# One matmul of 512 columns where the hi and the lo half of a weight matrix took two of 256

## The chip, the cores and the metric

The kernel runs on one core of a Trainium2 chip. The metric is the device time of one execution in microseconds (us). TensorE is called PE in the profile, VectorE DVE, ScalarE ACT, GpSimd POOL, and SyncE SP.

## What is computed

Three layers follow one another on 8 x 3072 tokens of 256 features. The third is the one that the change touches.

```python
X = np.fft.rfft(x, axis=1); y = np.fft.irfft(X * F, n=S, axis=1)     # 1: filter along the tokens
e = argmax(x @ w_gate); out[i] = gate * (relu(x[i] @ w1[e]) @ w2[e]) # 2: 8 experts, capacity 768
h = x @ w_in                                                         # 3: 256 -> 2048
g = np.maximum(h, 0.0) + np.log1p(np.exp(-np.abs(h)))                #    softplus
return g @ w_out                                                     #    2048 -> 256
```

## The kernel before

Only tokens that get one of the 6144 places of layer 2 need layers 2 and 3 in full. They are worked through in 16 **units** of 384 tokens (8 experts, two halves each); `units[v]` is unit v. Matrix products of layers 2 and 3 are done three times, in a 4-byte matmul format called fp32r: every operand is split into a part hi and a rest lo, and hi x hi, hi x lo and lo x hi are summed in PSUM.

For each unit the third layer runs over KI = 16 **chunks** of 128 hidden features. `wi(i)` makes the pre-activation `pi` of chunk i (six matmuls of 384 columns). ACT takes Abs, Exp and Ln of it, DVE adds `max(h, 0)` (`g`), ACT rounds to `gh`, and POOL subtracts to get `gl`. `wo(i)`, four steps later, multiplies with the chunk's 256 columns of `w_out`: for each of the three groups of 128 tokens (t = 0, 1, 2) it runs gh x woh, gh x wol and gl x woh, nine matmuls of 256 columns. They sum into `po` over all 16 chunks. `po` lies in two PSUM banks (pool `pso`): tokens t = 0 and 1 in the two halves of the first, t = 2 in the second. After chunk 15 `take` copies the three sums to SBUF tiles `ot` on DVE, and `store` scatters them to the output from POOL's queue. The next unit's `wo(0)` writes the same two banks, so its first matmul waits for `take`.

The program is one list of steps. Unit v's chunk i has step 16 v + i, and events of one step are put out in the order W2, WI, SP, WO, SUM, W1, TAKE. Between `wo(15)` of a unit (step 16 v + 19) and `wo(0)` of the next (step 16 v + 20) PE therefore runs one `w1` block (`pw`), one `w2` block (`py`) and one `wi` block (`pi`), each of six matmuls of 384 columns; these `w1` and `w2` blocks belong to the second layer of later units. DVE gets `hl`, the rest that belongs to that `w1` block, ahead of `take`. From unit 13 on no `w1` or `w2` is left, and only `wi` lies between.

`P.pv` is another PSUM pool, of one bank. It is scratch space of the conversion of `w_in` and `w_out` (`split_res`) and idle after that.

Of the kernel before, what the change touches and what calls it, by code (L numbers as in the profile page):

```python
# [7 lines left out]
F32 = mybir.dt.float32  # L8
F32R = mybir.dt.float32r
# [3 lines left out]
ALU = mybir.AluOpType  # L13
# [4 lines left out]
NB, S, D, E = 8, 3072, 256, 8  # L18
# [183 lines left out]
def body(tc, cap, x, ff, fx, wg, w1, w2, win, wout, m1, m2, m3, m4, small, out):  # L202
    nc = tc.nc
# [5 lines left out]
    KI = DFF // 128  # L209
# [10 lines left out]
    pso = ctx.enter_context(tc.tile_pool(name="pso", bufs=2, space=PSUM))  # L220
# [18 lines left out]
    ts = const.tile([128, nblk], F32, name="ts")  # L239
# [352 lines left out]
    def left_pools(st, tag):  # L592
        pool = lambda n, b: st.enter_context(tc.tile_pool(name=tag + n, bufs=b, reuse_waits="tile"))
        P.g = pool("g", 4)
        P.sp = pool("sp", 3)
        P.o = pool("o", 7)
        wp = pool("wo", 1)
        P.woh = wp.tile([128, KI, D], F32R, name="woh")
        P.wol = wp.tile([128, KI, D], F32R, name="wol")

    def load_res(q, which):
        t = P.wl.tile([128, 512], mybir.dt.int64 if f64 else F32, name="wst", tag="wst", bufs=3)
# [3 lines left out]
    def split_res(q, which, space):  # L606

        t = P.res.pop((q, which))  # L610

        def parts():
            if which == 0:
                return (w[q].rearrange("p b k f -> p (b k f)") for w in (P.wih, P.wil))
            return (w[:, 2 * q:2 * q + 2].rearrange("p b c -> p (b c)") for w in (P.woh, P.wol))

        if f64:
            two = t.bitcast(U32).rearrange("p (f two) -> p f two", two=2)
            lw, hw = two[:, :, 0], two[:, :, 1]
            if space is None:  # L620
                v = P.wl.tile([128, 512], U32, name="wv", tag="wv", bufs=1)
            else:
                pool, tag = space()
                v = pool.tile([128, 512], U32, name="pv", tag=tag)
            f = P.wl.tile([128, 512], F32, name="wf", tag="wf")
            nc.vector.tensor_scalar(v, hw, 0xFFFFF, 0x100000, op0=ALU.bitwise_and, op1=ALU.bitwise_or)
            nc.vector.scalar_tensor_tensor(out=f, in0=lw, scalar=2.0 ** -32, in1=v, op0=ALU.mult, op1=ALU.add)
            nc.vector.tensor_scalar(v, hw, 0x7FF00000, None, op0=ALU.bitwise_and)
            yield 0
            nc.scalar.activation(out=v, in_=v, func=ACTF.Relu, scale=8.0, bias=ebias)  # L630
            yield 1
            nc.vector.scalar_tensor_tensor(out=v, in0=hw, scalar=0x80000000, in1=v,
                                           op0=ALU.bitwise_and, op1=ALU.bitwise_or)
            nc.vector.scalar_tensor_tensor(out=f, in0=f, scalar=2.0 ** -20, in1=v.bitcast(F32),
                                           op0=ALU.mult, op1=ALU.mult)
            yield 2
        else:
            f = t
            yield 0
            yield 1  # L640
            yield 2
        hi, lo = parts()
        nc.scalar.copy(hi, f)
        yield 3
        nc.gpsimd.tensor_tensor(out=lo, in0=f, in1=hi.bitcast(F32), op=ALU.subtract)
# [17 lines left out]
    class Unit:  # L663
# [148 lines left out]
            self.sp_h(i)  # L812
            self.sp_l(i)

        def wo(self, i):
            if i == 0:
                po = [pso.tile([128, 2, D], F32, name="po", tag="o") for _ in range(2)]
                self.po = [po[0][:, 0], po[0][:, 1], po[1][:, 0]]
            gh, gl = self.g.pop(i)
            for t in range(3):  # L820
                ts = slice(t * 128, t * 128 + 128)
                for n, (a, b) in enumerate(((gh, P.woh), (gh, P.wol), (gl, P.woh))):
                    nc.tensor.matmul(self.po[t], lhsT=a[:, ts], rhs=b[:, i], skip_group_check=True,  # L823
                                     start=(i == 0 and n == 0 and t != 1), stop=(i == KI - 1 and n == 2))

        def take(self):
            self.ot = []
            for t in range(3):
                ot = P.o.tile([128, D], F32, name="ot", tag="ot")
                nc.vector.tensor_copy(ot, self.po[t])  # L830
                self.ot.append(ot)

        def store(self, group, tiles=range(3)):
# [9 lines left out]
    class Rest:  # L843


        def sums(self, k, c):
            if not k and not c:
                self.s = P.o.tile([128, 2, D], F32, name="cs", tag="cs", bufs=1)
            cs = slice(32 * c, 32 * c + 32)
            src = (P.woh, P.wol)[k].bitcast(F32)[:, :, cs].rearrange("p k c -> p c k")  # L850
            nc.vector.tensor_reduce(out=self.s[:, k, cs], in_=src, axis=AXL.X, op=ALU.add)

        def zero(self):
# [21 lines left out]
    with tc.manual_schedule():  # L875
# [17 lines left out]
        units = [Unit(e, h) for h in range(nunit) for e in range(E)]  # L893
# [46 lines left out]
        for g in range(8):  # L940
            for h in range(2):
                n = "x1", g, h
                add(n, "PE", 896, lambda g=g, h=h: cv.x1(0, g, h), after=["m1", "warm", ("x", 0, g)],
                    take=["a", "e1"] if g + h == 0 else ["a"], give=[("xt", ("x", 0, g))],
# [4 lines left out]
        for k in range(12):  # L949
            n = "tr1", k  # L950
# [3 lines left out]
        for b in range(1, STATIC):  # L954
            for g in range(8):
                for i in range(2):
                    n = "xo", b, g, i
                    add(n, "PE", 856, lambda b=b, g=g, i=i: cv.x1_out(b, g, i), after=["m1", ("x", b, g)],
                        take=["a"] if i else ["a", "s1"], give=[("xt", ("x", b, g))], behind=[("xo", b, g, 0)] if i else [])
# [10 lines left out]
        for b in range(STATIC):  # L970
            for k in range(12):
                s2, tf, zs, s3, se = (("s2", b, k // 2), *((x, b, k) for x in ("tf", "zs", "s3", "se")))
                prev = lambda x, n=12, k=k: [(x, b, k - 1)] if k else [(x, b - 1, n - 1)] if b else []
                if k % 2 == 0:
# [7 lines left out]
                    take=["o"] if k else ["o", f"e{b % 2}"], give=[("z", tf)], behind=prev("s3"))  # L982
# [3 lines left out]
            for h in range(2):  # L986
                n = "gs", b, h
                add(n, "PE", 1000, lambda b=b, h=h: cv.gsum(b, h), after=es + ["const"], take=["o"], give=[e0])
                add(("gx", b, h), ("DVE", "ACT")[h], 520, lambda b=b, h=h: cv.gsum_x(b, h), after=[n],
                    take=["gx"] if h == 0 else [], give=[("o", n)], behind=[("gx", b, 0)] if h else [])  # L990
            for t in range(2):
                n = "gt", b, t
# [3 lines left out]
                    take=["gsb"] if t == 0 else [], give=[("a", n)], behind=[("gg", b, 0)] if t else [])  # L996
# [34 lines left out]
            for m in range(16):  # L1031
# [7 lines left out]
                    take=["o"] if m % 2 else ["o", "yt"], give=[("j", tr)], behind=prev("s4"))  # L1039
# [43 lines left out]
        def left_room():  # L1083
            stl.close()
            left_pools(stm, "M")
# [9 lines left out]
        W2, WI, SP, WO, SUM, W1, TAKE, TR, AHEAD = range(9)  # L1095
# [21 lines left out]
        for v in range(HEAD):  # L1117
            u = units[v]
# [4 lines left out]
            for k in range(2):  # L1123
                n = "pt", v, k
# [5 lines left out]
            for j in range(8):  # L1130
                if v > 1 and 16 * (v - 2) + 2 * j - 3 >= STEPS:
                    continue
                n = "w1", v, j
                add(n, "PE", 1044, lambda u=u, j=j: u.w1_p(j), after=[("xl", v, 0), ("xl", v, 1), ("wl", v, j // 2)],
                    take=["a"], give=[("x", ("xh", v, 0)), ("w1h", ("wh", v, j // 2))],
# [3 lines left out]
                if v < 2 or 16 * (v - 2) + 2 * j < STEPS:  # L1139
# [3 lines left out]
                        take=["yy", "yy"] if j == 0 else [],  # L1143
                        give=[("h", ("hh", v, j)), ("w2h", ("wh", v, 4 + j // 2))], tail=2000)
            for d in range(2 if ("w2", v, 7) in plan.node else 0):
                add(("yh", v, d), "ACT", 490, lambda u=u, d=d: u.y_h(d), after=[("w2", v, 7), "low"],
                    take=["Y"] if d == 0 else [], behind=[("yh", v, 0)] if d else [])
# [7 lines left out]
        for n, (q, which) in enumerate(res):  # L1155
            kind = (n >= TURN[0]) + (n >= TURN[1])
            tag = "yov"[kind]
# [11 lines left out]
        def prior(*n):  # L1169
            return [n] if n in plan.node else []  # L1170

        for v, u in enumerate(units):
            for i in range(KI):
                t = 16 * v + i
                wi, ab, su, gh, gl, wo = ((x, v, i) for x in ("wi", "ab", "su", "gh", "gl", "wo"))
                if t < STEPS:
                    add(wi, "PE", 1044, lambda u=u, i=i: u.wi(i), after=[("yl", v, 0), ("yl", v, 1), ("c", i // 2, 4), "left"],
                        take=["a"], give=[("Y", ("yh", v, 0))], behind=prior("wi", *((v, i - 1) if i else (v - 1, KI - 1))))
# [5 lines left out]
                if t + 4 < STEPS:  # L1184
                    add(wo, "PE", 1075, lambda u=u, i=i: u.wo(i), after=[gl, ("c", KI // 2 + i // 2, 4)],
                        take=["o"] * 2 * (i == 0), give=[("gg", gh)],
# [21 lines left out]
        def ev(t, order, fn, *args):  # L1208
            if t < STEPS:
                return  # L1210
            at.setdefault(t, []).append((order, len(at.get(t, ())), fn, args))
# [19 lines left out]
        for v, u in enumerate(units):  # L1231
            b = 16 * (v - 2)
            if v >= HEAD:
                ev(b - 16, AHEAD, load_x, u)
                for k in range(2):
                    ev(b - 7 + 2 * k, TR, u.tr_x, k)
            for j in range(8 if v > 1 else 0):
                ev(b + 2 * j - 3, W1, u.w1, j)
                ev(b + 2 * j, W2, u.w2, j)
            for i in range(KI):  # L1240
                t = 16 * v + i
                ev(t, WI, u.wi, i)
                ev(t + 2, SP - 0.5, u.sp_split, i)
                ev(t, SP, u.sp_act, i)
                ev(t, SUM, u.sp_sum, i)
                ev(t + 4, WO, u.wo, i)
            ev(16 * v + 19, TAKE, u.take)
            for t in range(3):
                ev(max(16 * v + 21, 46 + 3 * v) + t * (v < len(units) - 1), AHEAD, u.store, "out", [t])
            ev(16 * v + 13, AHEAD, nc.gpsimd.drain)  # L1250
# [15 lines left out]
    with tc.If(fv > 0):  # L1266
# [53 lines left out]
        with ExitStack() as st:  # L1320
            wi_pools(st, "G")
            right_pools(st, "G")
            low_pool(st, "G")
            left_pools(st, "G")
            for k in range(2):
                for q in range(KI // 2):
                    load_res(q, k)
                    for _ in split_res(q, k, None):
                        pass
            with tc.For_i(0, E, 1) as e:  # L1330
                with tc.For_i(0, nunit, 1) as h:
                    u = Unit(e, h)
# [77 lines left out]
```

## Time and profile before

| | |
|---|---|
| time, median of 3 runs | 1044.64 us (1044.56 to 1045.86) |
| profiled execution | 1043.66 us, of which its span is 1041.9 us |
| PE busy | 1023.2 us, 98% of the span, 7112 matmuls |
| ACT, POOL, DVE busy | 777.7, 597.1, 468.1 us |
| granted PE clock, mean | 0.999 of full speed |
| `po` matmuls (L823) | 3 x 768 of 256 columns |
| `ot` copies (L830) | 48, 17.2 us in all |

The chain that ended last goes through PE for 90% of the span. Matmuls overlap in the pipeline, so the duration of one (282 ns for 256 columns) says little; what one costs a busy PE is read from the distance between starts.

### The profile page before, as it was taken

The numbers are of one execution on the slowest core, as the hardware profiler recorded it, in microseconds if no ns is written. First come the engines' busy times: TensorE is split into PE (matmuls) and PEld (weight loads), VectorE is DVE, ScalarE is ACT, GpSimd is POOL, SyncE is SP. The second block draws the span as 40 slices with busy tenths as digits, with TensorE's granted clock in tenths as the row PEclk, the third lists the DMA queues.
The fourth block names the chain that finished last, engine by engine and source line by source line (L and its number), as shares of the span: only waits on it lengthen the run. The fifth ranks groups of instructions, "written<-read, shape, count | busy, mean of one in ns | idle before, by whom it ended". The sixth has DMA issues, their size and how long they took to land.

```text
span 1041.9 us, 19044 instructions
## 1 busy us (share of the span) xinstructions
PE 1023.2 (98%) x7112; PEld 951.2 (91%) x7112; DVE 468.1 (45%) x895; ACT 777.7 (75%) x1612; POOL 597.1 (57%) x560
## 2 busy tenths in 40 slices
PE   9999999999999999999999999999999999999997
PEld 7655676699999999999999999999999999999996
DVE  3855899888856332323233333232333333322222
ACT  4465568778877787878787878787878787877885
POOL 0502544688754658665656565656565656554554
PEclk9999999999999999999999999999999999999999
DMA  9967727654211662333323333321121212100000
GB/s 291 297 214 235 246 87 249 220 178 137 71 47 41 203 258 83 135 107 112 122 92 122 111 102 112 122 92 61 51 63 51 64 51 66 46 11 6 17 16 19
DMA packets 72823, 120.04 MB, mean 115 GB/s; under 512 B 6928, under 2 KB 46736, under 8 KB 72720
## 3 DMA queue, kind: packets, MB, share of 16 engines
q1 hardware_dynamic: 65424, 96.69, 28.9%
q0 software_dynamic: 4608, 12.59, 3.5%
q10 hardware_dynamic: 2688, 9.44, 2.7%
q8 instruction: 58, 0.95, 0.4%
q14 instruction: 45, 0.37, 0.1%
HBM read 71.51 MB, written 47.19 MB: 114 GB/s over the span
## 4 chain that ended last, share of the span: by engine, by line
PE 90%; POOL 2%; DMA 2%; issue 2%; DVE 2%; ACT 1%; POOLq 0%; ACTq 0%; DVEq 0%; SPq 0%
PE pi L791 24%; PE po L823 24%; PE pw L737 13%; PE py L766 12%; PE p L437 3%; PE p L385 2%; PE p L332 2%; PE p L398 2%; PE p L309 1%; PE p L357 1%; POOL gl L808 1%; DMA xt<-in_x_dram 1%; PE pt L714 1%; PE p L536 1%; DMA fi<-in_fx_dram 1%
## 5 line engine op out<-in xcount | busy, mean ns | idle before, releaser
L657 DVE SCALAR_TENSOR_TENSOR g<-pi,ln 128x384 f32<-128x384 f32 x256 | 142.4, 557 | 488.5 <-ACT ln L652 447.2
L808 POOL TENSOR_TENSOR gl<-g,gh 128x384 fp32r<-128x384 f32 x256 | 259.9, 1018 | 114.8 <-ACT gh L803 109.0
L823 PE MATMUL po<-woh,gh 128*128 128x256 f32 x768 | 216.5, 282 | 1.9 <-DVE ot L830 1.9
L823 PE MATMUL po<-woh,gl 128*128 128x256 f32 x768 | 216.3, 282 | 1.0 <-POOL gl L808 1.0
L823 PE MATMUL po<-wol,gh 128*128 128x256 f32 x768 | 216.0, 281 | 0.0
L649 ACT ACTIVATE ab<-pi 128x384 f32<-128x384 f32 x256 | 124.7, 487 | 119.8 <-PE pi L791 113.2
L791 PE MATMUL pi<-yh,wih 128*128 128x384 f32 x512 | 172.7, 337 | 1.0 <-DVE g L657 1.0
L791 PE MATMUL pi<-yh,wil 128*128 128x384 f32 x512 | 173.2, 338 | 0.0
L791 PE MATMUL pi<-yl,wih 128*128 128x384 f32 x512 | 173.0, 338 | 0.0
L823 PEld LDWEIGHTS po<-woh,gh 128*128 128x128 f32 x768 | 144.0, 188 | 4.3 <-ACT ab L649 2.5
L823 PEld LDWEIGHTS po<-woh,gl 128*128 128x128 f32 x768 | 144.8, 189 | 1.2 <-POOL gl L808 1.2
L823 PEld LDWEIGHTS po<-wol,gh 128*128 128x128 f32 x768 | 145.1, 189 | 0.0
L652 ACT ACTIVATE ln<-ab 128x384 f32<-128x384 f32 (+1 forms) x257 | 134.9, 525 | 8.1
L650 ACT ACTIVATE ab<-ab 128x384 f32<-128x384 f32 (+1 forms) x257 | 134.8, 525 | 8.1
L689 POOL TENSOR_TENSOR w1l<-ws,w1h 128x512 fp32r<-128x512 f32 x64 | 82.9, 1296 | 98.0 <-ACT w1h L684 68.6
L803 ACT CAST gh<-g 128x384 fp32r<-128x384 f32 x256 | 130.0, 508 | 0.7 <-DVE g L657 0.5
L689 POOL TENSOR_TENSOR w2l<-ws,w2h 128x512 fp32r<-128x512 f32 x64 | 82.9, 1296 | 74.9 <-ACT w2h L684 73.6
L791 PEld LDWEIGHTS pi<-yh,wih 128*128 128x128 f32 x512 | 96.2, 188 | 1.3 <-DVE g L657 1.3
L791 PEld LDWEIGHTS pi<-yh,wil 128*128 128x128 f32 x512 | 96.3, 188 | 0.0
L791 PEld LDWEIGHTS pi<-yl,wih 128*128 128x128 f32 x512 | 96.2, 188 | 0.0
L377 POOL TENSOR_TENSOR z<-z,t 128x512 f32<-128x512 f32 x36 | 45.8, 1273 | 75.8 <-DVE t L372 59.9
L766 PE MATMUL py<-hh,w2h 128*128 128x384 f32 x256 | 88.5, 346 | 0.0
(140 smaller groups left out, 1894.8 us busy)
## 6 DMA issues: line engine op xcount, KB each, us to landing
ws<-in_w_dram SPq DMA_DIRECT2D x128, 256.0 KB, 2.9
out_dram<-cs SPq DMA_DIRECT2D x48, 512.0 KB, 4.1
xt<-in_x_dram SPq DMA_DIRECT2D x24, 384.0 KB, 7.1
mid<-s ACTq DMA_DIRECT2D x16, 384.0 KB, 4.3
rowsd<-yt SPq DMA_DIRECT2D x16, 384.0 KB, 3.9
it<-mid SPq DMA_DIRECT2D x24, 256.0 KB, 4.4
wst<-in_win_dram SPq DMA_DIRECT2D x8, 512.0 KB, 6.0
wst<-in_wout_dram SPq DMA_DIRECT2D x8, 512.0 KB, 3.5
```

Of the source, the lines that this page charges most:

```text
L377: nc.gpsimd.tensor_tensor(out=z, in0=z, in1=t2, op=ALU.add)
L649: nc.scalar.activation(out=ab[:, :n], in_=h, func=ACTF.Abs)
L650: nc.scalar.activation(out=ab[:, :n], in_=ab[:, :n], func=ACTF.Exp, scale=-1.0)
L652: nc.scalar.activation(out=ln[:, :n], in_=ab[:, :n], func=ACTF.Ln, bias=1.0)
L657: nc.vector.scalar_tensor_tensor(out=g[:, :n], in0=h, scalar=0.0, in1=ln[:, :n], op0=ALU.max, op1=ALU.add)
L689: nc.gpsimd.tensor_tensor(out=lo, in0=self.ws.pop(i), in1=hi.bitcast(F32), op=ALU.subtract)
L737: nc.tensor.matmul(ps, lhsT=a[:, k, fs], rhs=b[:, k], start=(n == 0), stop=(n == 5))
L766: nc.tensor.matmul(self.py[d], lhsT=a[:, j % 2, ds], rhs=b, start=(j == 0 and n == 0), stop=(j == 7 and n == 2))
L791: nc.tensor.matmul(pi, lhsT=a[i // 2][:, i % 2, k], rhs=b[:, k], start=(n == 0), stop=(n == 5))
L803: nc.scalar.copy(gh, self.g[i])
L808: nc.gpsimd.tensor_tensor(out=gl, in0=g, in1=gh.bitcast(F32), op=ALU.subtract)
L823: nc.tensor.matmul(self.po[t], lhsT=a[:, ts], rhs=b[:, i], skip_group_check=True, start=(i == 0 and n == 0 and t != 1), stop=(i == KI - 1 ...
```

## The change

`woh` and `wol` become one tile `wo`, in which each chunk's 256 columns of hi are followed by its 256 columns of lo. From unit 1 on, `wo(i)` multiplies gh with both in one matmul of 512 columns and then gl with the hi half: six matmuls for nine, over as many columns. Each token group has a PSUM bank to itself, the third from `P.pv`, and its sum stands there in two halves. `take` copies the first half of a bank to `ot` and adds the second to it, on DVE; in the last unit ACT does the copy. Unit 0 keeps the nine matmuls and the plain copies.

```diff
-        P.woh = wp.tile([128, KI, D], F32R, name="woh")
-        P.wol = wp.tile([128, KI, D], F32R, name="wol")
+        P.wo = wp.tile([128, KI, 2, D], F32R, name="wo")
...
-        def wo(self, i):
-            if i == 0:
+        def wo(self, i, wide=False):
+            if i == 0 and wide:
+                po = [pso.tile([128, 2, D], F32, name="po", tag="o") for _ in range(2)]
+                self.po = po + [P.pv.tile([128, 2, D], F32, name="pq", tag="v")]
+            elif i == 0:
...
+                if wide:
+                    nc.tensor.matmul(self.po[t].rearrange("p k c -> p (k c)"), lhsT=gh[:, ts], skip_group_check=True,
+                                     rhs=P.wo[:, i].rearrange("p k c -> p (k c)"), start=(i == 0), stop=(i == KI - 1))
+                    nc.tensor.matmul(self.po[t][:, 0], lhsT=gl[:, ts], rhs=P.wo[:, i, 0], skip_group_check=True,
+                                     start=False, stop=(i == KI - 1))
+                    continue
...
-        def take(self):
+        def take(self, wide=False):
...
+                if wide:
+                    (nc.scalar.copy if self is units[-1] else nc.vector.tensor_copy)(ot, self.po[t][:, 0])
+                    nc.vector.tensor_tensor(out=ot, in0=ot, in1=self.po[t][:, 1], op=ALU.add)
+                else:
+                    nc.vector.tensor_copy(ot, self.po[t])
...
-                ev(t + 4, WO, u.wo, i)
-            ev(16 * v + 19, TAKE, u.take)
+                ev(t + 4, WO, u.wo, i, v > 0)
+            ev(16 * v + 19, TAKE, u.take, v > 0)
```

The order of all other work is the same on every engine. On PE, at the start of a unit (here unit 2; `pi` is the `wi` block ahead of it, `po` are the products with w_out), the rows before are these, with what each matmul waits for:

```order
L791 MATMUL pi<-yh,wil_1315 128x384
L823 MATMUL po<-woh,gh 128x256 [waits DVE_49,Activation_49]
L823 MATMUL po<-wol,gh 128x256
L823 MATMUL po<-woh,gl 128x256 [waits Pool_49]
L823 MATMUL po<-woh,gh 128x256
L823 MATMUL po<-wol,gh 128x256
L823 MATMUL po<-woh,gl 128x256
L823 MATMUL po<-woh,gh 128x256 [waits DVE_49]
L823 MATMUL po<-wol,gh 128x256
L823 MATMUL po<-woh,gl 128x256
```

The same place of the changed kernel (`pq` is the sum in the third bank):

```order
L792 MATMUL pi<-yh,wil_1315 128x384
L827 MATMUL po<-wo,gh 128x512 [waits DVE_49,PE_49,Activation_49]
L829 MATMUL po<-wo,gl 128x256 [waits Pool_49]
L827 MATMUL po<-wo,gh 128x512 [waits DVE_49,PE_49]
L829 MATMUL po<-wo,gl 128x256
L827 MATMUL pq<-wo,gh 128x512 [waits DVE_49,PE_49]
L829 MATMUL pq<-wo,gl 128x256
```

Two waits for DVE have become three, one for each token group. On DVE, `take` of a unit stands behind the `hl` of the `w1` block. Before:

```order
L749 SCALAR_TENSOR_TENSOR hl<-pw,hh 128x384 [waits Activation_49]
L830 COPY ot<-po 128x256 [waits PE_49]
L830 COPY ot<-po 128x256 [waits DMASW2_49]
L830 COPY ot<-po 128x256 [waits DMASW3_49,PE_49]
L657 SCALAR_TENSOR_TENSOR g<-pi,ln 128x384 [waits Activation_49,Pool_49] x2
```

And in the changed kernel:

```order
L750 SCALAR_TENSOR_TENSOR hl<-pw,hh 128x384 [waits Activation_49]
L841 COPY ot<-po 128x256 [waits PE_49]
L842 TENSOR_TENSOR ot<-ot,po 128x256 [waits DVE_49]
L841 COPY ot<-po 128x256 [waits DMASW2_49,PE_49]
L842 TENSOR_TENSOR ot<-ot,po 128x256 [waits DVE_49]
L841 COPY ot<-pq 128x256 [waits DMASW3_49,PE_49]
L842 TENSOR_TENSOR ot<-ot,pq 128x256 [waits DVE_49]
L658 SCALAR_TENSOR_TENSOR g<-pi,ln 128x384 [waits Activation_49,Pool_49] x2
```

Three instructions have become six at the same place, and each sum waits for the copy ahead of it on DVE itself.

## Rows read from the trace of the kernel before

**Rows 1.** The page's chain that ended last: shares of the span, by engine, by line

```profile
PE 90%; POOL 2%; DMA 2%; issue 2%; DVE 2%; ACT 1%; POOLq 0%; ACTq 0%; DVEq 0%; SPq 0%
PE pi L791 24%; PE po L823 24%; PE pw L737 13%; PE py L766 12%; PE p L437 3%; PE p L385 2%; PE p L332 2%; PE p L398 2%; PE p L309 1%; PE p L357 1%; POOL gl L808 1%; DMA xt<-in_x_dram 1%; PE pt L714 1%; PE p L536 1%; DMA fi<-in_fx_dram 1%
```

**Rows 2.** Stretches: busy us of PE, PEld, DVE, ACT, POOL; clock, DMA

```profile
500.00:600.00 100.00, 100.00 (x668) 99.59 (x667) 31.53 (x60) 78.28 (x165) 62.43 (x59) 1.00 0.33 113
975.00:1000.00 25.00, 25.00 (x178) 25.00 (x177) 6.63 (x12) 22.78 (x48) 13.59 (x15) 1.00 0.03 11
```

**Rows 3.** PE's waits: for whom, us in total, times, longest

```profile
PE po L823 <- DVE ot L830: 1.9, 2, 1.0
```

**Rows 4.** Timeline of PE, first matmul of each block: start, duration

```profile
602.12 0.34 PE L791 MATMUL pi<-yh,wih 128*128 128x384 f32 x1
...
603.16 0.28 PE L823 MATMUL po<-woh,gh 128*128 128x256 f32 x1
...
604.23 0.34 PE L791 MATMUL pi<-yh,wih 128*128 128x384 f32 x1
...
605.30 0.28 PE L823 MATMUL po<-woh,gh 128*128 128x256 f32 x1
...
606.36 0.34 PE L737 MATMUL pw<-xh,w1h 128*128 128x384 f32 x1
...
607.43 0.34 PE L766 MATMUL py<-hh,w2h 128*128 128x384 f32 x1
...
608.47 0.33 PE L791 MATMUL pi<-yh,wih 128*128 128x384 f32 x1
```

**Rows 5.** Timeline of DVE at the end of unit 6

```profile
614.97 1.08 DVE L830 COPY ot<-po 128x256 f32<-128x256 f32 x3
617.77 0.56 DVE L657 SCALAR_TENSOR_TENSOR g<-pi,ln 128x384 f32<-128x384 f32 x1 [1.72 <-ACT ln L652]
```

**Rows 6.** Timeline of PE at the same place

```profile
615.68 0.34 PE L791 MATMUL pi<-yh,wil 128*128 128x384 f32 x1
615.86 0.36 PE L823 MATMUL po<-woh,gh 128*128 128x256 f32 x1
616.06 0.28 PE L823 MATMUL po<-wol,gh 128*128 128x256 f32 x1
...
617.00 0.34 PE L791 MATMUL pi<-yh,wih 128*128 128x384 f32 x1
```

**Rows 7.** Timelines of DVE and PE at the end of unit 13

```profile
968.92 1.08 DVE L830 COPY ot<-po 128x256 f32<-128x256 f32 x3
...
969.81 0.36 PE L823 MATMUL po<-woh,gh 128*128 128x256 f32 x1 [0.97 <-DVE ot L830]
970.00 0.28 PE L823 MATMUL po<-wol,gh 128*128 128x256 f32 x1
...
970.95 0.34 PE L791 MATMUL pi<-yh,wih 128*128 128x384 f32 x1
...
972.00 0.28 PE L823 MATMUL po<-woh,gh 128*128 128x256 f32 x1
```

**Rows 8.** Single lines (duration min/median/max), and DVE's timeline in layer 2's gate

```profile
L830 DVE COPY ot<-po x48: 411/414/424, 302.4 to 1034.6; 128x256 f32<-128x256 f32 x48
155.43 0.41 DVE L497 TENSOR_TENSOR rk<-rk,pb 96x256 f32<-96x256 f32 x1
155.87 0.42 DVE L500 TENSOR_TENSOR v<-rk,oh 96x256 f32<-96x256 f32 x1
156.32 0.59 DVE L503 TENSOR_REDUCE ixf<-v 96x32 f32<-96x256 f32 x1
```

**Rows 9.** Timelines of DVE and POOL at the program's end

```profile
1033.88 1.09 DVE L830 COPY ot<-po 128x256 f32<-128x256 f32 x3 [2.75 <-PE po L823]
...
1034.59 1.00 POOL L835 DMA_INDIRECT out_dram<-ot,si  x1 [1.65 <-DVE ot L830]
...
1037.18 0.98 POOL L835 DMA_INDIRECT out_dram<-ot,si  x1 [0.30 <-issue]
```

More of the change, by code (lines that the diff above doesn't have):

```diff
@@ L614, in parts @@
                 return (w[q].rearrange("p b k f -> p (b k f)") for w in (P.wih, P.wil))
-            return (w[:, 2 * q:2 * q + 2].rearrange("p b c -> p (b c)") for w in (P.woh, P.wol))
+            return (P.wo[:, 2 * q:2 * q + 2, k] for k in range(2))
         if f64:
@@ L642, in split_res @@
         hi, lo = parts()
+        if which:
+            f = f.rearrange("p (b c) -> p b c", b=2)
         nc.scalar.copy(hi, f)
@@ L821, in wo @@
                 ts = slice(t * 128, t * 128 + 128)
-                for n, (a, b) in enumerate(((gh, P.woh), (gh, P.wol), (gl, P.woh))):
-                    nc.tensor.matmul(self.po[t], lhsT=a[:, ts], rhs=b[:, i], skip_group_check=True,
+                if wide:
[4 more added lines that the diff above has]
+                    continue
+                for n, (a, k) in enumerate(((gh, 0), (gh, 1), (gl, 0))):
+                    nc.tensor.matmul(self.po[t], lhsT=a[:, ts], rhs=P.wo[:, i, k], skip_group_check=True,
                                      start=(i == 0 and n == 0 and t != 1), stop=(i == KI - 1 and n == 2))
-        def take(self):
+        def take(self, wide=False):
             self.ot = []
@@ L829, in take @@
                 ot = P.o.tile([128, D], F32, name="ot", tag="ot")
-                nc.vector.tensor_copy(ot, self.po[t])
+                if wide:
[3 more added lines that the diff above has]
+                    nc.vector.tensor_copy(ot, self.po[t])
                 self.ot.append(ot)
@@ L849, in sums @@
             cs = slice(32 * c, 32 * c + 32)
-            src = (P.woh, P.wol)[k].bitcast(F32)[:, :, cs].rearrange("p k c -> p c k")
+            src = P.wo.bitcast(F32)[:, :, k, cs].rearrange("p k c -> p c k")
             nc.vector.tensor_reduce(out=self.s[:, k, cs], in_=src, axis=AXL.X, op=ALU.add)
```

## The prediction

> **What bounds the kernel now.** I read the chain that ended last first: it runs through PE for 90% of the span, and the products with w_out (L823) and with w_in (L791) hold 24% each [rows 1]. The stretches say the same of the part that the change touches: from 500 to 600 us PE is busy without a gap while ACT, the next engine, has 78 of 100 us, and late in the program, where only `wi` and `wo` are left, ACT has 22.8 of 25 [rows 2]. PE hardly waits, in all 1.9 us for `take`, in two places [rows 3]. So what the change saves on PE is saved in full, and every new wait of PE is paid in full. The reader should look for two things: the distance between matmul starts, and what PE meets at the start of a unit.
>
> **What PE pays for a chunk.** Nine matmuls of 256 columns lie between 603.16 and 604.23, the next nine between 605.30 and 606.36 [rows 4]: 1.065 us, or 118 ns each, where 256 columns at 2.4 GHz (the level that the granted clock of 1.00 in these stretches stands for) are 107 ns [rows 2]. A block of six matmuls of 384 columns takes 1.04 us when it follows another such block (602.12 to 603.16, 607.43 to 608.47), 173 ns each, where the columns alone are 160; it takes 1.07 us when it follows `wo` (604.23 to 605.30, 606.36 to 607.43) [rows 4].
>
> **Merged matmuls.** The columns stay: 3 x (512 + 256) are 9 x 256. What can go is the part of a matmul that doesn't come from columns, and the trace has no fp32r matmul of 512. The nearest rows give two ways to it: the 13 ns by which 384 columns exceed their streaming time, added to 213 ns, make 226; the line through 256 (118) and 384 (173.5) goes on to 229. I take 229, since that line rests on both widths. A chunk is then 3 x (229 + 118) = 1041 ns instead of 1065, 24 ns less. Of the 240 wide chunks (units 1 to 15), 14 stand at a boundary, which I cost as a whole below; 226 x 24 ns = 5.4 us. The bounds: a 512 as long as the two 256 that it replaces (236 ns) saves nothing; one at its bare streaming time (213 ns) saves 3 x 23 x 226 = 15.6 us.
>
> The Trainium skill's page "TensorE: Matmul & The Clock Gate", section "Back-to-back issue gap", puts a warm matmul at N/2.4 + 2.5 ns. By it a pair of 256 (2 x 109.2) against one 512 (215.8) is worth 2.6 ns, 1.8 us in all, so that hardly anything could be had by merging; the rows above differ from it, with 118 ns for 256 columns and 173 for 384.
>
> **The block behind it.** Each chunk is followed by one block of 384 columns, and that block is the slow one, 1.07 against 1.04 us [rows 4]. It is slow whether it is `wi` or `w1`, so it is not its operands but the nine short matmuls ahead of it. One place shows that this can go away: behind the chunk ahead of which PE had stood still for 0.97 us, the block takes 1.05 (970.95 to 972.00) [rows 7]. This looks like a supply of matmuls and weight loads that nine short matmuls run down and a pause, or longer matmuls, fill again. Six matmuls in a wide chunk's 1.04 us are as many as a 384 block has, so I expect most of it back: 240 x 30 ns = 7.2 us if all, 240 x 20 = 4.8 if as much as behind the pause. I take 6.0; the bounds are 0 and 7.2.
>
> **The boundary.** Here the change costs. Call T the start of `take` on DVE. Before, three copies run with starts 0.333 us apart (1.08 less one copy's 0.414, halved) [rows 5, 8]. The first matmul of the next unit waits for the two copies of the first bank, so until T + 0.333 + 0.414 = T + 0.75. It is recorded at T + 0.89 (615.86 against 614.97), but the one behind it follows after 0.20 us instead of 0.12, so it streams from about T + 0.97 [rows 5, 6]: 0.22 us pass between a copy's end and a streaming matmul. PE would have got there at T + 0.89 by itself (615.68 plus 0.18) [rows 6]. So this place has no slack today: the release comes 0.08 us late, and the chunk takes 1.14 us (615.86 to 617.00) [rows 6]. The 12 boundaries behind units 1 to 12 lie alike, T from 356.03 to 924.21, since `take` stands behind the `hl` of the `w1` block that PE itself does just ahead. Behind units 13 and 14 no such block is left, PE is there earlier and waits for the whole of it, but the first matmul again comes at T + 0.89 (969.81 against 968.92) [rows 7].
>
> After, each token group needs a copy and an add that waits for it. The gate has the same thing on 256 columns: an add with one operand in PSUM (`rk`, 0.42 us), and behind it an instruction that needs its result, which starts 0.44 to 0.45 us after it [rows 8]. So the add starts at T + 0.45 and ends 0.42 later, and the next, independent copy starts 0.335 after the add. The three adds end at T + 0.87, T + 1.65 and T + 2.44; the matmuls of the three groups may stream from T + 1.09, T + 1.87 and T + 2.66. PE needs only 0.347 us for a group (229 + 118 ns), so it waits again for the second and for the third, and ends the chunk at T + 2.66 + 0.35 = T + 3.01. Before it ended it at T + 0.89 + 1.14 = T + 2.03. That is 0.98 us for each of 14 boundaries, **13.7 us**. Nothing hides it: PE runs in order, and the `wi` behind it has to stand in the queue. Bounds: 0.85 us (a dependent start 0.03 and a release 0.02 quicker, three times or so), 11.9 us in all; 1.1 us, 15.4 us in all, if the added waits in PE's queue cost 0.05 each.
>
> DVE itself has room. Behind units 1 to 12 the next `g` starts at T + 2.80 (617.77) and waits for ACT [rows 5]; DVE is free by T + 2.4. Behind 13 and 14 `g` will be up to 0.7 us late, but what needs it is a `wo` four steps on. Unit 1's first chunk follows unit 0's plain copies and gains no wait.
>
> **The end.** The last unit's three scatters stand 1.3 us apart on POOL (1034.59 to 1037.18) and start with the first `ot` [rows 9]. Its sum has two steps now, ACT's copy and DVE's add, some 0.45 us more. But today the first copy waits for both token groups of its bank (1033.88); with a bank of its own, group 0 is released some 4 matmuls of 118 ns earlier, 0.47 us. I cost it at nothing, within 0.3 us.
>
> **The sum.** 13.7 - 5.4 - 6.0 = +2.3 us. On the profiled execution (1043.66 us, 1.0 below the median of the runs) that is 1045.9 us, on the median 1044.64 it is **1046.9 us**. This stands on the edge of what a measurement of this kernel can tell from no change, about 0.2% or 2.1 us.
>
> **Rivals.**
> *The merged matmul runs near its streaming time: faster.* If the excess over the columns is a price of the 256 and 384 widths that 512 hardly has, say 216 ns, a pair saves 20 ns: 3 x 20 x 226 = 13.6 us, and the sum is 13.7 - 13.6 - 6.0 = -5.9, 1038.7 us. It decides from 225 ns on: there 3 x 11.4 x 226 makes 7.7 us, which with the 6.0 equals the boundary. Against it speaks that the excess grows from 11 to 13 ns with the width [rows 4]. The 215.8 ns of the Trainium skill's page named above, for 512 columns, would be this case, if that figure held here while its 109.2 for 256 does not.
> *The slow block stays: clearly slower.* If it is the matmul of 256 columns just ahead, and not their number, that slows the next block, three of six remain and nothing comes back: 13.7 - 5.4 = +8.3, 1052.9 us. For it speaks that after the pause the `wo` matmuls themselves still ran at 118 to 120 ns (970.95 less 970.00, eight matmuls) [rows 7], so a full supply did not quicken them.
> *No change to be told.* With the whole 7.2 us back and 512 columns at 226 ns (33 ns a chunk, 7.5 us) the sum is 13.7 - 7.5 - 7.2 = -1.0, 1043.6 us. Nothing in the trace parts this from my own forecast; it is its lower edge.
>
> **How the numbers follow.** The forecast, all terms near their values (1043.0 to 1050.0), gets 0.56: 0.33 of it within 0.2%, 0.23 above. The slow block staying gets 0.22, all slower. The quick 512 gets 0.22, all faster. So faster 0.22, same 0.33, slower 0.45. The range takes in most of both rivals: 1040.0 to 1053.5 us leaves out the quick 512 below 218 ns, and a boundary at its upper bound together with a block that stays slow.
>
> **What the profile will show.** Right: the first three wide matmuls of a unit (L827) wait for DVE at three places, with 0.4 to 0.5 us ahead of the second and third, some 0.9 to 1.0 us a unit, and 13 us or so in PE's waits where 1.9 stood; starts of 512 columns 226 to 230 ns apart from the next matmul's; blocks of 384 behind `wo` at 1.04 us. Wrong, towards faster: 512 columns under 225 ns, or adds that start without waiting the copy out, so that the second and third group find their banks free. Wrong, towards slower: blocks behind `wo` still at 1.07, or one wait for the last add ahead of all three groups, which would hold PE until T + 2.66 with its whole 1.04 us still to do, 23 us in place of 13.7.

## The result and the profile after

The changed kernel takes **1053.51 us** (median of 6 runs, 1053.04 to 1056.9) where the kernel before takes 1044.6 (6 runs, 1043.31 to 1045.88): the ratio is 1.009, with a 95% interval of 1.0074 to 1.0105. It is slower by 8.9 us. The forecast was 1046.9, and the range ended at 1053.5. The profiled execution took 1053.66 us, its span is 1051.8 us and its mean granted clock 0.997.

The page of the changed kernel: PE's row, and the chain that ended last by engine and by line, to be held against [rows 1].

```profile
PE 1026.6 (98%) x6392; PEld 912.0 (87%) x6392; DVE 485.9 (46%) x937; ACT 780.2 (74%) x1615; POOL 596.9 (57%) x560
...
PE 90%; DVE 4%; issue 2%; ACT 1%; POOL 1%; POOLq 0%; ACTq 0%; DVEq 0%
PE pi L792 24%; PE pw L738 13%; PE py L767 11%; PE po L827 9%; PE pq L827 6%; PE po L829 5%; PE p L437 3%; PE p L385 3%; PE pq L829 3%; PE p L332 3%; PE p L357 2%; PE p L398 2%; DVE ot L841 2%; PE po L833 2%; PE p L309 1%
```

There are 720 matmuls fewer (6392 for 7112), and PE is busy for longer. DVE's share of the chain has doubled, and `ot` is now a line of it. The same stretch as in [rows 2]: busy us of PE, PEld, DVE, ACT, POOL, the granted clock and the DMA engines' share.

```profile
500.00:600.00 100.00, 99.18 (x566) 93.14 (x565) 33.05 (x64) 76.42 (x160) 63.22 (x59) 1.00 0.32 109
```

PE, which had no gap there, has one now. PE's waits name it: for whom, us in total, times, longest.

```profile
PE pq L827 <- DVE ot L842: 2.9, 14, 0.2
PE po L827 <- DVE ot L842: 2.8, 14, 0.2
PE po L827 <- ACT ab L651: 2.3, 2, 1.1
```

Where 1.9 us stood [rows 3], these are 8.0. The third row names ACT, but its two waits, behind units 13 and 14, end at T + 1.01 (T is the start of `take` on DVE, as in the prediction), where PE's first matmul starts at every boundary, 0.15 us after the first add has ended: they are waits for `ot` too. The 8.0 us are still less than what the boundaries cost, as the timelines of one of them tell. First DVE at the end of a unit, then PE (start, duration, engine, line, operation, idle time ahead of it).

```profile
619.44 0.41 DVE L841 COPY ot<-po 128x256 f32<-128x256 f32 x1
619.88 0.42 DVE L842 TENSOR_TENSOR ot<-ot,po 128x256 f32<-128x256 f32 x1
620.22 0.42 DVE L841 COPY ot<-po 128x256 f32<-128x256 f32 x1
620.67 0.42 DVE L842 TENSOR_TENSOR ot<-ot,po 128x256 f32<-128x256 f32 x1
621.01 0.42 DVE L841 COPY ot<-pq 128x256 f32<-128x256 f32 x1
621.46 0.42 DVE L842 TENSOR_TENSOR ot<-ot,pq 128x256 f32<-128x256 f32 x1
```

```profile
620.14 0.34 PE L792 MATMUL pi<-yh,wil 128*128 128x384 f32 x1
620.45 0.47 PE L827 MATMUL po<-wo,gh 128*128 128x512 f32 x1
620.75 0.28 PE L829 MATMUL po<-wo,gl 128*128 128x256 f32 x1
621.24 0.47 PE L827 MATMUL po<-wo,gh 128*128 128x512 f32 x1 [0.20 <-DVE ot L842]
621.55 0.28 PE L829 MATMUL po<-wo,gl 128*128 128x256 f32 x1
622.03 0.47 PE L827 MATMUL pq<-wo,gh 128*128 128x512 f32 x1 [0.21 <-DVE ot L842]
622.34 0.28 PE L829 MATMUL pq<-wo,gl 128*128 128x256 f32 x1
622.45 0.34 PE L792 MATMUL pi<-yh,wih 128*128 128x384 f32 x1
```

T is 619.44. The adds start at T + 0.44, 1.23 and 2.02, the last ends at T + 2.44, and the chunk ends at T + 3.01 (622.45), as it does at all 14 boundaries, within 0.01. Two matmuls of 512 columns with one of 256 between stand 0.79 us apart here, and 0.34 in an ordinary chunk (below): 0.45 us are lost ahead of the second group and as much ahead of the third. The view of waits shows only 0.20 of it, since a waiting matmul is also recorded as longer (0.47 us for 0.40) and the one before it is recorded with 0.28 us where the next can start 0.11 behind it. Distances between starts show the whole.

An ordinary chunk of the changed kernel (PE):

```profile
627.71 0.39 PE L827 MATMUL po<-wo,gh 128*128 128x512 f32 x1
627.93 0.28 PE L829 MATMUL po<-wo,gl 128*128 128x256 f32 x1
628.05 0.40 PE L827 MATMUL po<-wo,gh 128*128 128x512 f32 x1
628.28 0.28 PE L829 MATMUL po<-wo,gl 128*128 128x256 f32 x1
628.40 0.40 PE L827 MATMUL pq<-wo,gh 128*128 128x512 f32 x1
628.64 0.29 PE L829 MATMUL pq<-wo,gl 128*128 128x256 f32 x1
628.76 0.34 PE L792 MATMUL pi<-yh,wih 128*128 128x384 f32 x1
...
629.80 0.39 PE L827 MATMUL po<-wo,gh 128*128 128x512 f32 x1
```

The chunk takes 1.05 us and the block behind it 1.04, against 1.065 and 1.07 in [rows 4]. The block has come down as forecast; the chunk hardly has. In the trace's records, which are finer than the view's 10 ns, the medians over some 230 chunks are these (start to next start, ns):

| kernel | matmuls of a chunk, in order | chunk | block behind |
|---|---|---|---|
| before | 115 122 117, 118 117 118, 119 121 117 | 1063 | 1070 |
| after | 229 113, 233 117, 241 125 | 1058 | 1043 |

In units 3 to 11 one chunk is longer than that: the last one, ahead of the boundary. Here are PE and POOL there, at the end of unit 6.

```profile
616.04 0.40 PE L827 MATMUL po<-wo,gh 128*128 128x512 f32 x1
616.28 0.37 PE L829 MATMUL po<-wo,gl 128*128 128x256 f32 x1
616.49 0.40 PE L827 MATMUL po<-wo,gh 128*128 128x512 f32 x1
...
617.18 0.34 PE L738 MATMUL pw<-xh,w1h 128*128 128x384 f32 x1
```

```profile
610.06 1.29 POOL L690 TENSOR_TENSOR w1l<-ws,w1h 128x512 fp32r<-128x512 f32 x1 [2.29 <-ACT w1h L685]
...
615.19 2.00 POOL L809 TENSOR_TENSOR gl<-g,gh 128x384 fp32r<-128x384 f32 x2
```

The same place before, POOL and then PE:

```profile
605.55 1.30 POOL L689 TENSOR_TENSOR w1l<-ws,w1h 128x512 fp32r<-128x512 f32 x1 [2.29 <-ACT w1h L684]
...
610.68 2.00 POOL L808 TENSOR_TENSOR gl<-g,gh 128x384 fp32r<-128x384 f32 x2
```

```profile
611.64 0.28 PE L823 MATMUL po<-woh,gh 128*128 128x256 f32 x1
```

POOL does `w1l`, three gathers of `xd` and then two `gl`, the first of which is ready after about half of its row, at 616.2. From `w1l` to `gl` this takes 5.13 us (610.06 to 615.19), and before it took as much (605.55 to 610.68). But PE comes to this chunk 5.98 us after `w1l`'s start (616.04), where it came 6.09 us after it before (605.55 to 611.64): it has run three quicker chunks and blocks in between. The `gl` that was just in time is now late. The second matmul needs it: it is recorded at 0.37 us instead of 0.28, and the next stands 0.21 us behind it, not 0.12. The chunk takes 1.14 us (616.04 to 617.18), and 1.14 to 1.16 in each of the nine units. In units 1, 12, 13 and 14 the last chunk takes the ordinary 1.06. In unit 2 it waits over a microsecond for `gl` in both kernels, 2.34 us before and 2.43 after.

### The profile page after: what moved, and what is told of

It reads as the page before. It is cut to its first block, busy times and chain, and to the rows that moved or that the text cites. A ratio compares the mean times of both kernels' runs of the same rounds, so it can differ in the third digit from the quotient of the medians.

```text
span 1051.8 us, 17698 instructions
## 1 busy us (share of the span) xinstructions
PE 1026.6 (98%) x6392; PEld 912.0 (87%) x6392; DVE 485.9 (46%) x937; ACT 780.2 (74%) x1615; POOL 596.9 (57%) x560
## 4 chain that ended last, share of the span: by engine, by line
PE 90%; DVE 4%; issue 2%; ACT 1%; POOL 1%; POOLq 0%; ACTq 0%; DVEq 0%
PE pi L792 24%; PE pw L738 13%; PE py L767 11%; PE po L827 9%; PE pq L827 6%; PE po L829 5%; PE p L437 3%; PE p L385 3%; PE pq L829 3%; PE p L332 3%; PE p L357 2%; PE p L398 2%; DVE ot L841 2%; PE po L833 2%; PE p L309 1%
## 5 line engine op out<-in xcount | busy, mean ns | idle before, releaser
L827 PE MATMUL po<-wo,gh 128*128 128x512 f32 x480 | 180.5, 398 | 5.1 <-DVE ot L842 2.8
L829 PE MATMUL po<-wo,gl 128*128 128x256 f32 x480 | 135.2, 282 | 1.1 <-POOL gl L809 1.1
L827 PEld LDWEIGHTS po<-wo,gh 128*128 128x128 f32 x480 | 90.0, 187 | 22.0 <-issue 10.0
L827 PE MATMUL pq<-wo,gh 128*128 128x512 f32 x240 | 97.5, 406 | 2.9 <-DVE ot L842 2.9
L829 PEld LDWEIGHTS po<-wo,gl 128*128 128x128 f32 x480 | 90.3, 188 | 3.5 <-POOL gl L809 3.4
L745 ACT ACTIVATE hh<-pw 128x384 fp32r<-128x384 f32 x128 | 62.9, 492 | 33.3 <-PE pw L738 31.4
```

What stands on the lines that cost most here:

```text
L827: nc.tensor.matmul(self.po[t].rearrange("p k c -> p (k c)"), lhsT=gh[:, ts], skip_group_check=True, rhs=P.wo[:, i].rearrange("p k c -> p ( ...
L829: nc.tensor.matmul(self.po[t][:, 0], lhsT=gl[:, ts], rhs=P.wo[:, i, 0], skip_group_check=True, start=False, stop=(i == KI - 1))
```

## The experiments

Two theories stood against each other after the result. The first is the prediction's own account of the boundary with a smaller gain from the merge: the boundary costs its 13.7 us, and the merged matmuls save less than was forecast. The rival puts the loss into the merged matmuls or the third bank themselves, wherever they stand, so that a free boundary would not bring the time below that of before. Later runs asked why the chunk is no shorter. One reading (P) was that two matmuls into the same bank follow one another more slowly; the other (S) that it costs something to go from long matmuls to short ones or back. Each ratio is to the kernel before as it ran beside that experiment; its medians there lie between 1045.3 and 1045.6 us, against 1044.6 in the result, so medians of experiments that ran apart compare to about 1 us.

**take_early: the sums are taken a step's worth earlier.** In the changed kernel, `take` is put out directly behind its unit's last chunk, ahead of the `w1` block and its `hl`.

```diff
-        W2, WI, SP, WO, SUM, W1, TAKE, TR, AHEAD = range(9)
+        W2, WI, SP, WO, SUM, W1, TR, AHEAD = range(8)
+        TAKE = WO + 0.5
```

> The changed kernel, but take stands ahead of the sum g and of hl in its step, so that DVE starts it as soon as the last products of the unit are done, one PE block of 1.07 us earlier. Theory A (the copy-and-add chain on DVE, begun only behind hl, holds PE about 1.07 us at each of 14 boundaries): the waits for the adds go, the 12 boundaries with w1 and w2 between become free, those behind units 13 and 14 keep some 0.4 us; 1053.5 - 15 = 1038.5 us (1037 to 1040). Theory B (the merged matmuls themselves, or the third bank, cost the time): at least 1050 us.

Measured: **1037.18 us**, ratio 0.9918 (0.9901 to 0.9935) to the kernel before. DVE and then PE at the start of a unit:

```profile
611.44 0.41 DVE L841 COPY ot<-po 128x256 f32<-128x256 f32 x1
...
613.47 0.42 DVE L842 TENSOR_TENSOR ot<-ot,pq 128x256 f32<-128x256 f32 x1
```

```profile
615.04 0.39 PE L827 MATMUL po<-wo,gh 128*128 128x512 f32 x1
...
616.10 0.34 PE L792 MATMUL pi<-yh,wih 128*128 128x384 f32 x1
```

The first `wo` comes at T + 3.60, 1.1 us after the last add, and the chunk takes its ordinary 1.06 us. In the changed kernel the boundary chunk, which PE could have begun at 620.31, ended 1.08 us late, twelve times, and 2.2 us late behind units 13 and 14; in this one those two lose 0.4 each. 12 x 1.08 + 2 x 1.8 = 16.6 us, and the medians differ by 16.3. The boundary is more than the whole loss, and the rival falls. `g` and `hl` behind the sums are later on DVE, and PE waits for neither.

**copies_only: the adds left out.** `take` copies only the first half of each bank; the output lacks gh times the lo half of w_out in units 1 to 15.

```diff
-                    (nc.scalar.copy if self is units[-1] else nc.vector.tensor_copy)(ot, self.po[t][:, 0])
-                    nc.vector.tensor_tensor(out=ot, in0=ot, in1=self.po[t][:, 1], op=ALU.add)
+                    nc.vector.tensor_copy(ot, self.po[t][:, 0])
```

> The changed kernel, but take copies only the first half of each bank (it leaves out adding gh times the lo half of w_out): three copies as before the change, each bank released by its own copy. Theory A: releases at T + 0.63, 0.97, 1.30 us against needs at T + 0.89, 1.24, 1.58, so no wait at 12 boundaries and a shorter one at two; 1053.5 - 15.5 = 1038 us. Theory B: at least 1050 us.

Measured: 1036.48 us, ratio 0.9917 (0.99 to 0.9933). What PE waits for `ot` is back to two places.

```profile
PE po L827 <- DVE ot L841: 1.4, 2, 0.7
```

At 12 boundaries the chunk ends at T + 1.94, 1.07 us before the changed kernel's T + 3.01. The third bank and the three separate waits cost nothing by themselves; the adds do.

**copies_first: three copies, then three adds.** No add has to wait out the copy just ahead of it.

```diff
-            self.ot = []
+            self.ot = [P.o.tile([128, D], F32, name="ot", tag="ot") for _ in range(3)]
             for t in range(3):
...
+            for t in range(3 if wide else 0):
+                nc.vector.tensor_tensor(out=self.ot[t], in0=self.ot[t], in1=self.po[t][:, 1], op=ALU.add)
```

> The changed kernel, take in its place behind hl, but the three copies first and then the three adds. Theory A as a model of DVE: no add has to wait a copy out, the adds end at T + 1.42, 1.76 and 2.09 us instead of T + 0.87, 1.65 and 2.44, PE ends the first chunk at T + 2.68 instead of T + 3.02: 14 x 0.34 = 4.8 us less than the changed kernel, 1048.7 us. If PE's loss at the boundary had another cause than the end of each group's add: no change, 1053.5 us.

Measured: 1048.48 us, ratio 1.0029 (1.0019 to 1.0039). DVE, then PE; a row with x2 holds two operations.

```profile
615.79 0.75 DVE L840 COPY ot<-po 128x256 f32<-128x256 f32 x2
616.45 0.41 DVE L840 COPY ot<-pq 128x256 f32<-128x256 f32 x1
616.78 0.74 DVE L844 TENSOR_TENSOR ot<-ot,po 128x256 f32<-128x256 f32 x2
617.44 0.42 DVE L844 TENSOR_TENSOR ot<-ot,pq 128x256 f32<-128x256 f32 x1
```

```profile
617.34 0.47 PE L827 MATMUL po<-wo,gh 128*128 128x512 f32 x1 [0.50 <-DVE ot L844]
...
618.46 0.34 PE L792 MATMUL pi<-yh,wih 128*128 128x384 f32 x1
```

Six operations 0.33 us apart end at T + 2.07 in place of T + 2.44, and the chunk at T + 2.67, 0.34 us sooner: 14 x 0.34 = 4.8 us, and the medians differ by 5.0. The account of DVE in the prediction holds here too.

**nine: the merge alone undone.** The changed kernel with its three banks, halves and adds, but nine matmuls of 256 columns.

```diff
-                    nc.tensor.matmul(self.po[t].rearrange("p k c -> p (k c)"), lhsT=gh[:, ts], skip_group_check=True,
...
+                    for n, (a, k) in enumerate(((gh, 0), (gh, 1), (gl, 0))):
+                        nc.tensor.matmul(self.po[t][:, k], lhsT=a[:, ts], rhs=P.wo[:, i, k], skip_group_check=True,
```

> The changed kernel with the three banks, the interleaved weights and the copy-and-add take, but nine matmuls of 256 columns again (gh x hi and gl x hi into the first half of a bank, gh x lo into the second). Theory A (the merge itself saves about 33 ns a chunk, 5 in the chunk and 27 in the block behind it): the block behind goes back to 1.07 us and the time rises by 226 x 33 ns = 7.5 us to 1061 us. Theory B (512 columns cost more than two times 256): 1053 us or less.

Measured: 1059.78 us, ratio 1.0137 (1.012 to 1.0154). Chunk and block are those of before again, 1063 and 1070 ns. So the merge is worth 6.3 us on the medians, and nearly all of it lies in the block behind the chunk (27 ns), hardly any in the chunk (5 ns).

**before_early: the kernel before, with the earlier `take`** (the edit of take_early).

> The kernel before (nine matmuls, plain copies) with take ahead of g and hl in its step, as in take_early: the control for what the place of take is worth without the merge. Theory A: only what the trace of before shows at its boundaries can go, 12 x 0.08 us and most of 2 x 1.0 us behind units 13 and 14: some 2.5 to 3 us faster than before, 1042.5 us, and take_early stands 5 to 8 us below it (240 x 32 ns = 7.7 us for the merge). If the early place were worth more than that by itself (theory B), before_early would come to 1038 us or less.

Measured: 1041.94 us, ratio 0.9964 (0.9952 to 0.9977). Even the plain copies had cost some 3 us at their place. With the early `take` in both, the merge brings 1041.94 to 1037.18: it gains 4.8 us, just under the 5 to 8 expected. The traces show what the chunks and blocks saved and the time did not: take_early still loses 0.4 us behind each of units 13 and 14 (before_early nothing), 0.8 us in all to the late `gl` of last chunks, and 0.6 us from the last matmul to the end of the program.

**rotated: no two neighbours in one bank.** take_early, with the groups' matmuls in the order 512 of t = 0, 256 of 1, 512 of 2, 256 of 0, 512 of 1, 256 of 2.

```diff
+            if wide and i:
+                for j in range(6):
+                    t, ts = j % 3, slice(j % 3 * 128, j % 3 * 128 + 128)
+                    if j % 2 == 0:
...
```

> take_early with the six matmuls of a chunk (from chunk 1 on) in the order 512 of group 0, 256 of group 1, 512 of group 2, 256 of group 0, 512 of group 1, 256 of group 2: long and short still alternate, but no two neighbours write the same PSUM bank. Theory P (a matmul that adds into the bank that the one just ahead wrote is held up): 1032 ns a chunk as in gl_last, 1031 to 1034 us. Theory S (what slows a matmul is the short ones ahead of it): 1058 ns as in take_early, 1036 to 1038 us.

Measured: 1036.41 us, ratio 0.9913 (0.9896 to 0.993). The chunk is 228 113 232 118 241 125, in all 1058 ns, as without the rotation. P falls.

**nine_spread: nine matmuls, neighbours in different banks**, with the earlier `take`.

```diff
+                for n, (a, k) in enumerate(((gh, 0), (gh, 1), (gl, 0))):
+                    for t in range(3):
```

> nine, with the early take, and the nine matmuls of 256 columns ordered so that neighbours write different banks (gh x hi for the three groups, then gh x lo, then gl x hi). Theory P: the 1063 ns of a chunk fall to 9 x 113 = 1017 ns and the time to some 1032 us. Theory S: chunk 1063 and block behind 1070 ns as in before; with the boundaries free 1059.8 - 16 = 1044 us (1042 to 1045).

Measured: 1044.58 us, ratio 0.999 (0.9981 to 1.0). Chunk 1063, block behind it 1070 ns: nothing moved, which speaks against P a second time.

**gl_last: the three long ones first.** take_early, with three matmuls of 512 columns and then three of 256.

```diff
+            if wide:
+                for t in range(3):
+                    nc.tensor.matmul(self.po[t].rearrange("p k c -> p (k c)"), lhsT=gh[:, t * 128:t * 128 + 128], skip_group_check=True,
...
+                for t in range(3):
+                    nc.tensor.matmul(self.po[t][:, 0], lhsT=gl[:, t * 128:t * 128 + 128], rhs=P.wo[:, i, 0], skip_group_check=True,
...
+                return
```

> take_early, and within a chunk the three matmuls of 512 columns come first, then the three of 256. Theory S (a matmul is slowed by the short ones just ahead of it, which run down a supply): three times 229 and three times 117, 1038 ns a chunk against 1058, the block behind it somewhat slow again (1050 to 1060 against 1043), together some 3 us less than take_early. Theory C (the products with w_out have a price by their columns, in whatever order): chunk and time as take_early.

Measured: **1032.42 us**, ratio 0.9871 (0.9854 to 0.9888). PE in a chunk and the two blocks behind it:

```profile
640.03 0.62 PE L826 MATMUL po<-wo,gh 128*128 128x512 f32 x2
640.48 0.39 PE L826 MATMUL pq<-wo,gh 128*128 128x512 f32 x1
640.71 0.40 PE L829 MATMUL po<-wo,gl 128*128 128x256 f32 x2
...
641.06 0.34 PE L738 MATMUL pw<-xh,w1h 128*128 128x384 f32 x1
...
642.11 0.33 PE L767 MATMUL py<-hh,w2h 128*128 128x384 f32 x1
```

The chunk takes 1.03 us, in the records 228 227 227, 113 119 118 = 1032 ns, where the alternating order takes 1058; the block behind it takes 1048. Chunk and block together are 2080 ns for 2101, and 21 x 240 is 5.0 us, where 4.8 were measured. The last chunk of a unit also takes 1032 (but for unit 2): `gl` is needed 0.45 us later than in the alternating order, and POOL is done. Behind units 13 and 14 PE loses 1.15 us each, since all three groups must be free within the first 0.45 us.

**gl_first: the three short ones first** (the loops of gl_last the other way round, from the second chunk of a unit on).

> take_early with the order of gl_last turned round (from chunk 1 on): the three matmuls of 256 columns first, then the three of 512. Theory S in its form of now (matmuls behind a short one are slowed, more so when long and short alternate): as few changes between long and short as in gl_last, so chunk and block behind together about 2080 ns (gl_last 1032 + 1048), with some 10 ns of the price now on the 512s and none on the block behind: 1031 to 1034 us. If only a long matmul directly behind a single short one were dear, it would be the same; if it were the number of 256 in the chunk alone, 2101 ns and 1037 us.

Measured: 1040.06 us, ratio 0.995 (0.9933 to 0.9966). The 2080 ns of chunk and block and the 1031 to 1034 us did not come true. PE:

```profile
642.57 0.40 PE L826 MATMUL po<-wo,gl 128*128 128x256 f32 x2
...
642.92 0.63 PE L829 MATMUL po<-wo,gh 128*128 128x512 f32 x2
643.38 0.39 PE L829 MATMUL pq<-wo,gh 128*128 128x512 f32 x1
643.61 0.34 PE L792 MATMUL pi<-yh,wih 128*128 128x384 f32 x1
...
644.67 0.40 PE L826 MATMUL po<-wo,gl 128*128 128x256 f32 x2
```

It has as few changes between long and short as gl_last, and yet it costs as much as the alternating order: here 1.04 us for the chunk and 1.06 for the block, 2.10 together (in the records an ordinary pair lies between 2095 and 2105 ns). S, as a price for each change, falls as well. The 2101 ns that the expectation gave for a price by the number of 256 alone did come, but gl_last has as many of them and takes 2080. The time is 2.9 us above take_early for another reason: a chunk now begins with its `gl`. In units 3 to 11 the last chunk starts 0.22 us late and takes 0.10 us longer than the others, 2.9 us in all where take_early loses 0.8, and behind units 13 and 14 PE loses 0.65 us each where take_early loses 0.4.

**ends: gl_last, with the alternating order kept where a boundary has no slack**, in the first and last chunk of units 13 to 15.

```diff
-            if wide:
+            if wide and not (i in (0, KI - 1) and self in units[13:]):
```

> gl_last, but by group (512, 256, 512, 256, 512, 256) in chunks 0 and 15 of units 13 to 15, so that behind units 13 and 14, where only one block of 384 lies between, take can begin earlier and the first bank is wanted first: at each of the two places PE's loss should fall from 1.15 us (gl_last) to 0.42 (take_early). 1032.4 - 1.4 = 1031.0 us. The best version that the runs point to.

Measured: 1031.13 us, ratio 0.9863 (0.9847 to 0.9879), the shortest of all, though the interval overlaps that of gl_last. In its trace PE loses 0.42 us behind each of units 13 and 14, as expected, where gl_last lost 1.15. It beats the kernel before, which ran beside it, by 14.4 us, and the changed kernel by some 22.

## Why the prediction missed, step by step

**The boundary** was forecast at 13.7 us, and it is 13.8: T + 3.01 at all 14 places where T + 2.03 stood. Each piece held: the dependent add 0.44 us after its copy's start, 0.22 us from an add's end to a streaming matmul, three waits rather than one. Where the waits would show was put wrong: not 13 us in the view of waits with 0.4 to 0.5 ahead of the second and third group, but 8.0 and 0.20, since that view does not show the whole of a wait.

**The block behind it** was forecast at 6.0 us. It came down by 27 ns, from 1070 to 1043: 226 x 27 = 6.1 us, counted without the 14 boundary chunks.

**Merged matmuls is the step that failed,** by its size: 5.4 us were forecast, from 229 + 118 ns a pair and 1041 a chunk. The chunk takes 1058 where 1063 stood, so 226 x 5 = 1.1 us. Behind a block of 384 columns the 512 is the 229 forecast. Behind a 256 it is 233 and 241, and the last 256 is 125. The forecast took one price for each width, from rows in which matmuls of one width follow one another; here they alternate. gl_last shows that the order matters: the same six matmuls with the long ones first have 227 ns for 512 columns and a chunk of 1032, less than forecast. It isn't the alternation alone, since gl_first, with the short ones first, has 230 to 234 ns for 512 columns and a chunk of 1047 to 1057. The lower bound of nothing, which the range held, was near the truth.

The Trainium skill, page "TensorE: Matmul & The Clock Gate", section "Back-to-back issue gap", gives N/2.4 + 2.5 ns for an isolated matmul, by which an estimate for 512 columns is 215.8. None of the measured distances in a busy TensorE, 227 to 241 ns, agrees with it. The prediction's inference from it, that merging itself brings little, held in the alternating order (5 ns a chunk) and not with the long ones first (31 ns).

**Left out** was the wait for `gl`. In units 3 to 11 the last chunk of a unit takes 1138 to 1161 ns, some 0.1 us more than the others, and in unit 2 it waits 0.1 us longer than before: 1.0 us in all. POOL's chain from `w1l` to `gl` is as long as before and PE is quicker to need it, so at this place PE hands back what it had gained over three chunks. The prediction looked at DVE and ACT for room, and not at POOL.

**The sum** with the measured terms is 13.8 + 1.0 - 1.1 - 6.1 = +7.6 us, where +2.3 was forecast: 4.3 of the 5.3 us between them are the merged matmuls, the rest `gl`. The traces agree: from unit 1's first `wo` matmul to the last one PE takes 738.2 us after (305.3 to 1043.5) and 730.6 before (303.3 to 1033.9), which is +7.6 too. From there to the end it is 8.3 us after and 8.0 before, so the end costs 0.3, as near to nothing as the prediction had it. The spans of the two profiled executions differ by 9.9 us, and the other 2.0 lie ahead of unit 1, where the change moves no work: unit 0's `take` starts at 302.4 us before and at 304.4 after. These come with the run and not with the change, as two experiments show that have the changed kernel's instructions up to there: copies_first starts it at 302.4, nine at 304.6. So the 1 us of the 8.9 that is left when 7.6 and 0.3 are taken off is most likely chance too: beside the experiments the kernel before had medians of 1045.3 to 1045.6, not 1044.6. One piece of it is the clock: from 196 to 206 us the granted clock was 1.00 in the profile before and 0.83 on the mean in the one after, where matmuls of `pw`, of 384 columns, stand 0.32 us apart (201.49 and 201.81), which is the 1.2 GHz level, and not 0.17; just ahead of them PE had waited 0.24 us for `xh`, as it had before.

```profile
196.00:206.00 10.00, 7.83 (x33) 6.25 (x33) 8.66 (x19) 6.27 (x13) 5.57 (x5) 0.83 0.76 258
```

In the same stretch before_early, which has the instructions of the kernel before there, was granted 0.83 as well, and copies_first 1.00. Before that spell too, PE stands 0.8 us later after than before (the first `pw` at 200.57 and 199.74); copies_first has it at 199.79, before_early at 200.73.

**The rivals.** The rival of the slow block named 1052.9 us, within a microsecond of the result, by a mechanism that did not occur: the block was quick, and the chunk was slow. The quick 512 (under 225 ns) did not occur either; the least median seen is 227.

**Open** is why the order of long and short matmuls matters. Chunk and block behind it take 2080 ns with the long ones first, 2101 alternating, some 2100 with the short ones first and 2133 with nine short ones. The same bank and a fixed price per change are ruled out. That something is run down by short matmuls and filled by long ones, as the prediction has it, fits 2133 and 2101; it doesn't say why three short ones at the start are worse than three at the end. Weight loads that run ahead, which the prediction names, are not seen in the records: from 620 to 950 us of before, after, gl_last and gl_first, 19 of 20 weight loads start 0 to 5 ns after the start of the matmul ahead of them, and none before it.

## What to carry to other kernels

On an engine that is never idle, a change that saves matmuls and adds steps to the release of their banks is decided at the release: follow it instruction by instruction (copy, dependent add, start of the next matmul), times the number of groups that wait apart, and then look whether the release can be put out earlier. Here moving six instructions ahead of a block on the queue turned +0.9% into -0.8%. What a matmul costs a busy TensorE depends on its neighbours' widths and on their order, so a price is taken from rows with the same neighbours in the same order; and what a quicker engine takes in is to be checked at the place where its producer is latest, not at the usual one.

## What the hardware showed beyond that

An fp32r matmul of 512 columns costs 227 ns among its like, 14 above its streaming time at 2.4 GHz (213), as 384 columns cost 173 with 13 above (160). The same six matmuls cost 1032 or 1058 ns by their order alone, at a granted clock of 1.00. A copy and an add on DVE that are independent start 0.33 us apart, and 0.45 when the add needs the copy's result.
